# Two PSUM banks taken in turn by the first-layer tiles and the small products of an attention-and-MLP kernel

## The chip, the cores and the metric

The kernel runs on one core of one Trainium2 chip. The metric is the device time of one execution in microseconds. Before the change it is 946.12 us, the median of 3 runs (945.28 to 949.42). A difference is told as a ratio of times measured in turn on one chip.

## The reference

Two computations stand behind each other. The first is clustered attention over 4 batches, 8 heads, 768 positions and 64 dimensions: each query and each key is assigned to the nearest of 16 centroids of its head, and a query sees only the keys of its own cluster.

```
mask   = q_assign[:, :, :, None] == k_assign[:, :, None, :]
scores = where(mask, scale * q @ k.T, -1e9)
x      = softmax(scores) @ v          # 4 x 768 rows of 512
```

The second is an MLP over the 3072 rows: `h = x @ w_in` (512 to 2048), `g = s * relu(h)**2 + b`, `out = g @ w_out` (2048 to 512). Everything is float32, and the kernel keeps that accuracy by splitting numbers into two float16 halves.

## The kernel before, in words

**Units and steps.** The attention is cut into 192 units (line 459): a unit is one batch, one chunk of 256 rows, one pair of heads, one of two row tiles and one head. Step `i` of the main loop issues unit `i`: its scores (`scores`, L476), the row maximum on VectorE (L486), the exponentials on ScalarE (L493, L496), the split into halves (ScalarE L126, GpSimd L528), the turn through a DMA transpose (L530), and four steps later the product with the values (`value`, L574 to L576).

**The MLP** runs behind it by `LAG = 21` steps. Its 192 steps are 12 chunks of 256 rows times 16 slices of the 2048 hidden columns. Step `m` makes one tile `h` (`mlp_in`, L632: 12 matmuls of 128x256 into one PSUM bank), ScalarE reads it once (`mlp_relu`, L639) and squares it twice from SBUF (L641, L642), GpSimd makes the low half (`mlp_gl`, L647), and two steps later 6 matmuls add it to the chunk's accumulator (`mlp_out`, L659). The first tile of a chunk needs the chunk's four `x` tiles, which `finish_x` makes.

**The small products** prepare later units and run as generators that `background()` moves on by one stage a step. `allmax` (L101, L102) takes a maximum over partitions with one or two matmuls against the identity: its tiles are `am_q`, `am_k`, `am_v` and `am_x`. `prep_k` and `prep_q` make `pk` and `pq`, the products of keys or queries with the centroids (L357, L358, L407, L408), which VectorE reads in `onehot` (L298, L299). `column_sums` makes one tile `pb` (L287).

**PSUM** has eight banks, and all are given away: four hold two score buffers, two hold the accumulator, one has the tag `h` and one the tag `m`.

```
    ps_s = ctx.enter_context(tc.tile_pool(name="ps_s", bufs=2, space=PSUM))
    ps_a = ctx.enter_context(tc.tile_pool(name="ps_a", bufs=1, space=PSUM))
    ps_h = ctx.enter_context(tc.tile_pool(name="ps_h", bufs=1, space=PSUM))
    ps_m = ctx.enter_context(tc.tile_pool(name="ps_m", bufs=1, space=PSUM))
```

A tag with one buffer holds one tile at a time. The next tile of the tag, in the order in which the code makes them, gets the bank when the last reader of the one before has finished. From step 21 on the `h` tiles alone use tag `h`, and the small products alone use tag `m`.

**The order of the work.** The code is written step by step, and the framework's scheduler (`schedule_with_timeline_sim=True`) then orders each engine's instructions by its own model of their times: what is ready earliest in the code's order goes first, with a few groups moved up by `high_priority`. On the chip each engine works its list in that fixed order, and a waiting instruction holds up all behind it on its engine.

Of the kernel before, what the change touches and what calls it, by code (L numbers as in the profile page):

```python
# [10 lines left out]
F32 = mybir.dt.float32  # L11
# [7 lines left out]
P = 128  # L19
# [7 lines left out]
def tile_cluster_attention_mlp(ctx, tc, q, k, v, cent, w_in, w_out, s_in, b_in, out):  # L27
# [15 lines left out]
    LAG = 21  # L43
# [10 lines left out]
    ps_h = ctx.enter_context(tc.tile_pool(name="ps_h", bufs=1, space=PSUM))  # L54
    ps_m = ctx.enter_context(tc.tile_pool(name="ps_m", bufs=1, space=PSUM))
# [35 lines left out]
    def columns(n, name):  # L91
        return sb.tile([P, n], BF16, tag=f"amb{n}", name=f"amb_{name}", bufs=3)

    def allmax(dst, src, name, bank="m"):
        n = src.shape[1]
        if bank == "turned":
            pm = turned[:, 0]
        else:
            pm = (ps_m if bank == "m" else ps_h).tile([P, 512], F32, tag=bank, name=f"am_{name}")
        for j in range(n):  # L100
            nc.tensor.matmul(pm[:, j * P : (j + 1) * P], src[:, j : j + 1].broadcast_to([P, P]), identb, start=True, stop=True)  # L101
        V.tensor_reduce(dst, pm[:, : n * P].rearrange("p (n q) -> p n q", q=P), axis=AX.X, op=ALU.max)  # L102
# [74 lines left out]
    def weight_tile(name):  # L177
        return cp.tile([P, KT, P], F32, tag="w", name=name, bufs=2 * NF + 1)
# [102 lines left out]
        WSP[ft] = (made[0], made[1].rearrange("p e a f -> p e (a f)"))  # L281

    def column_sums():
        pb = ps_m.tile([P, 512], F32, tag="m", name="pb")
        for ft in range(NF):
            for e in range(2):
                nc.tensor.matmul(pb, ones16, WSP[ft][1][:, e, :], start=(ft + e == 0), stop=(ft + e == NF))  # L287
        V.tensor_tensor(glob[:, 7:8], bv, glob[:, 4:5], op=ALU.mult)
        bias.append(weight_tile("bias").rearrange("p a f -> p (a f)"))
        V.tensor_scalar(bias[0], pb, glob[:, 7:8], None, op0=ALU.mult)  # L290
# [12 lines left out]
        V.tensor_tensor(o, e, m.unsqueeze(2).broadcast_to([P, nb, C]), op=ALU.is_equal)  # L303
        eng.tensor_scalar(dst, o.unsqueeze(2).broadcast_to([P, nb, 4, C]), mul, add, op0=ALU.mult, op1=ALU.add)

    step = [0]
    START = {b: [48 * b + x for x in ((-26, -25, -23, -20) if b == 1 else (-40, -38, -32, -28))] for b in range(1, B)}

    def until(k):
# [8 lines left out]
    def prep_k(b, hp):  # L318
        kb = kb_kept
        if b == 0 and hp > 0:  # L320
            kb = sb.tile([P, 2 * T, P], F16, tag="big", name=f"kb_{hp}", bufs=BIGN).rearrange("p (h t) (e d) -> p h t e d", h=2, e=2)
        n = f"{b}_{hp}"
        kn = sb.tile([P, 2, T, D], F32, tag="kv", name=f"kn_{n}", bufs=5)
        load(kn, k[b, 2 * hp : 2 * hp + 2].rearrange("h (p t) d -> p h t d", t=T))
        yield
        if b:
            yield from until(START[b][2] if hp == 0 else step[0] + 1)
        if hp == 0:
            KSM[b] = sb.tile([P, 4, NP], F32, tag="ksm", name=f"ksm_{n}", bufs=2)
        sm = [KSM[b][:, e, hp : hp + 1] for e in range(4)]  # L330
        km = columns(1, f"k{n}")
        absmax(km, kn.rearrange("p h t d -> p (h t d)"))
        if b:
            yield
        allmax(sm[1], km, f"k{n}", "m" if b or not hp else "h")
        yield
        scale2(sm[2], sm[1])
        inverse2(V, sm[3], sm[2], 22)
        if b == 0 and hp > 0:
            ka = sb.tile([P, 2 * T, P], F16, tag="big", name=f"ka_{hp}", bufs=BIGN).rearrange("p (h t) (e d) -> p h t e d", h=2, e=2)  # L340
        else:
            ka = sb.tile([P, 2, T, 2, D], F16, tag="big", name=f"ka_{n}", bufs=BIGN)
        yield from split(ka[:, :, :, 0, :], ka[:, :, :, 1, :], kn, sm[2], False)
        G.tensor_copy(kb[:, :, :, 0, :], ka[:, :, :, 0, :])
        KA = sb.tile([P, 2 * T, P], F16, tag="KA", name=f"KA_{n}", bufs=5)
        KB = sb.tile([P, 2 * T, P], F16, tag="KB", name=f"KB_{n}", bufs=5)
        KS[(b, hp)] = (KA, KB)
        last_turn[0] = nc.sync.dma_start_transpose(KA, ka.rearrange("p h t e d -> p (h t e d)"))
        yield
        yield  # L350
        pa = (ps_m if b or not hp else ps_h).tile([P, 512], F32, tag="m" if b or not hp else "h", name=f"pk_{n}")
        for h in range(2):
            hc = slice((2 * hp + h) * C, (2 * hp + h + 1) * C)
            for t in range(T):
                i = h * T + t
                o = pa[:, i * C : (i + 1) * C]
                nc.tensor.matmul(o, KA[:, i, :], cT[:, 0, hc], start=True, stop=False)  # L357
                nc.tensor.matmul(o, KA[:, i, :], cT[:, 1, hc], start=False, stop=True)  # L358
        mk = kb.rearrange("p h t e (r c) -> p (h t) e r c", c=C)[:, :, 1, :, :]
        yield from onehot(pa, 2 * T, f"k{n}", mk, BIG, -BIG, G if b or hp > 1 else V)  # L360
        last_turn[0] = nc.sync.dma_start_transpose(KB, kb.rearrange("p h t e d -> p (h t e d)"))

    def prep_q(b, c, hq):
        n = f"{b}_{c}_{hq}"
        nh = 4
        qn = sb.tile([P, 2 * T * P // 2], F32, tag="big", name=f"qn_{n}", bufs=BIGN)[:, : nh * CT * D].rearrange("p (h t d) -> p h t d", h=nh, t=CT)
        load(
            qn, q[b, nh * hq : nh * hq + nh].rearrange("h (p t) d -> p h t d", t=T)[:, :, c * CT : (c + 1) * CT, :]
        )
        yield  # L370
        prs = slice(2 * hq, 2 * hq + 2)
        sm = sb.tile([P, 4, 2], F32, tag="qsm", name=f"qsm_{n}", bufs=3)
        qm = columns(2, f"q{n}")
        absmax(qm, qn.rearrange("p (j h) t d -> p j (h t d)", j=2))
        if b + c:
            yield
        allmax(sm[:, 1, :], qm, f"q{n}", "m" if b or c else "h")
        yield
        f = sm[:, 2, :]
        scale2(f, sm[:, 1, :])  # L380
        V.tensor_tensor(f, f, KSM[b][:, 3, prs], op=ALU.min)
        V.tensor_tensor(sm[:, 1, :], f, KSM[b][:, 2, prs], op=ALU.mult)
        inverse2(V, sm[:, 3, :], sm[:, 1, :], -3)
        qa = sb.tile([P, 2 * T * P], F16, tag="big", name=f"qa_{n}", bufs=BIGN)[:, : nh * CT * 2 * D].rearrange("p (h t e d) -> p h t e d", h=nh, t=CT, e=2)
        qb = sb.tile([P, 2 * T * P], F16, tag="big", name=f"qb_{n}", bufs=BIGN)[:, : nh * CT * 2 * D].rearrange("p (h t e d) -> p h t e d", h=nh, t=CT, e=2)
        both = []
        for j in range(2):
            hs = slice(2 * j, 2 * j + 2)
            both.append(split(qb[:, hs, :, 0, :], qa[:, hs, :, 0, :], qn[:, hs], sm[:, 2, j : j + 1], b + c == 0))
        for z in zip(*both):  # L390
            yield
        for z in both:
            next(z, None)
        G.tensor_copy(qa[:, :, :, 1, :], qb[:, :, :, 0, :])
        QA = sb.tile([P, nh * CT, P], F16, tag="QA", name=f"QA_{n}", bufs=2)
        QB = sb.tile([P, nh * CT, P], F16, tag="QB", name=f"QB_{n}", bufs=2)
        QS[(b, c, hq)] = (QA, QB, sm)
        nc.sync.dma_start_transpose(QA, qa.rearrange("p h t e d -> p (h t e d)"))
        yield
        yield  # L400
        pa = (ps_m if b or c else ps_h).tile([P, 512], F32, tag="m" if b or c else "h", name=f"pq_{n}")
        for h in range(nh):
            hc = slice((nh * hq + h) * C, (nh * hq + h + 1) * C)
            for t in range(CT):
                i = h * CT + t
                o = pa[:, i * C : (i + 1) * C]
                nc.tensor.matmul(o, QA[:, i, :], cT[:, 0, hc], start=True, stop=False)  # L407
                nc.tensor.matmul(o, QA[:, i, :], cT[:, 2, hc], start=False, stop=True)  # L408
        mk = qb.rearrange("p h t e (r c) -> p (h t) e r c", c=C)[:, :, 1, :, :]
        yield from onehot(pa, nh * CT, f"q{n}", mk, BIG, 0.0, G if b or c or hq else V)  # L410
        nc.sync.dma_start_transpose(QB, qb.rearrange("p h t e d -> p (h t e d)"))
# [213 lines left out]

    def mlp_in(b, c, ft):
        n = f"{b}_{c}_{ft}"
        ph = ps_h.tile([P, 512], F32, tag="h", name=f"h_{n}")
        GS[(b, c, ft)] = ph
        terms = [(kt, wl, xl) for kt in range(KT) for wl, xl in ((0, 0), (0, 1), (1, 0))]  # L630
        for i, (kt, wl, xl) in enumerate(terms):
            nc.tensor.matmul(ph[:, :CW], WSP[ft][0][:, wl, kt, :], XS[(b, c, kt)][:, :, xl, :],  # L632
                             start=(i == 0), stop=(i == len(terms) - 1))
# [121 lines left out]
    while i < NU + 8 or i - LAG < NS + 4:  # L755
        m = i - LAG
# [66 lines left out]
```

## Time and profile before

| what | value |
|---|---|
| median of 3 runs | 946.12 us |
| the profiled execution | 952.97 us |
| its span, first to last instruction | 951.3 us |
| TensorE (PE) busy | 830.0 us, 87% of the span |
| ScalarE (ACT), VectorE (DVE), GpSimd (POOL) busy | 75%, 68%, 58% |
| `h` matmuls, L632 | 2304 in 192 tiles |
| accumulator matmuls, L659 | 1152 |

The profiled execution takes 1.7 us more than its span, and 6.85 us more than the median of the runs. Busy time counts matmuls from start to end, and they overlap, so a short gap between two of them can be hidden. A row of the timeline has the start, the length, the engine and line, the operation, what it writes and reads and how many are merged; in brackets stand the idle time of the engine before it and what ended that.

### The profile page before, as it was taken

Reading aid. Unit: us, or ns where it says so; the run is one execution under the profiler, and the core shown is the slowest. Engines: PE = TensorE matmul, PEld = TensorE weight load, DVE = VectorE, ACT = ScalarE, POOL = GpSimd, SP = SyncE. Lnnn points to the kernel's source line nnn. Section 1 sums busy time; section 2 is a strip of 40 time slices with the busy share of each in tenths; the row PEclk is TensorE's granted clock in tenths of the full one; section 3 lists DMA queues with packets and bytes.
Section 4 is the critical chain, followed back from the end, with each engine's and each line's share of the span. In section 5 each row is a group of like instructions: output and inputs, shape, how many; then the busy total and the mean of one; then the engine's idle time right before and its main releaser. Section 6 shows DMA issues by size and latency. Waiting matters only on the chain.

```text
span 951.3 us, 22936 instructions
## 1 busy us (share of the span) xinstructions
PE 830.0 (87%) x8697; PEld 580.1 (61%) x8697; DVE 651.1 (68%) x1684; ACT 715.4 (75%) x1405; POOL 548.0 (58%) x580
## 2 busy tenths in 40 slices
PE   0565667886999889999999989999999899999997
PEld 0353445554676657767666657667766676676764
DVE  7689978798786766758967766667877565654100
ACT  3469866777688678788878868888888788888543
POOL 3010115667577567677677747767776676666321
PEclk9975697999999999999999999999999999999999
DMA  5898513767897897876887978979968777577200
GB/s 165 215 262 283 161 38 80 174 145 150 168 168 146 172 204 123 167 162 139 178 169 164 201 156 148 171 145 197 178 140 182 145 123 159 115 140 140 46 23 23
DMA packets 437759, 144.25 MB, mean 152 GB/s; under 512 B 405392, under 2 KB 434064, under 8 KB 437648
## 3 DMA queue, kind: packets, MB, share of 16 engines
q1 hardware_dynamic: 437648, 142.78, 70.7%
q8 instruction: 68, 1.11, 0.5%
q14 instruction: 43, 0.35, 0.1%
HBM read 35.69 MB, written 6.29 MB: 44 GB/s over the span
## 4 chain that ended last, share of the span: by engine, by line
PE 45%; DVE 23%; DMA 12%; ACT 7%; issue 5%; POOL 2%; SPq 1%; POOLq 0%; DVEq 0%; ACTq 0%
PE h L632 16%; PE acc L659 16%; PE sc L476 6%; DVE ssm L486 5%; DMA qn<-in_q_dram 3%; DMA PT<-ph 2%; PE sc L574 2%; DMA kn<-in_k_dram 2%; DMA vn<-in_v_dram 2%; PE sc L576 2%; PE sc L575 2%; ACT p L496 1%; DVE wis L279 1%; DVE qa L196 1%; DMA wst<-in_moe_w_in_dram 1%
## 5 line engine op out<-in xcount | busy, mean ns | idle before, releaser
L528 POOL TENSOR_TENSOR ph<-p,ph 128x768 f16<-128x768 f32 x176 | 297.0, 1688 | 129.7 <-ACT ph L126 71.1
L632 PE MATMUL h<-x,wis 128*128 128x256 f16 x2304 | 291.9, 276 | 16.1 <-ACT r L639 9.7
L659 PE MATMUL acc<-wos,gs 128*128 128x512 f16 x1152 | 299.7, 381 | 4.1 <-POOL gs L647 2.8
L632 PEld LDWEIGHTS <-wis 128*128 128x128 f16 x2304 | 222.5, 99 | 72.3 <-issue 18.0
L496 ACT ACTIVATE p<-sc,ssm,qsm 128x768 f32<-128x768 f32 x192 | 188.5, 982 | 2.0
L647 POOL TENSOR_TENSOR gs<-r,gs 128x256 f16<-128x256 f32 x192 | 136.5, 712 | 88.1 <-ACT r L642 79.4
L486 DVE TENSOR_REDUCE ssm<-sc 128x1 f32<-128x768 f32 x192 | 181.7, 947 | 2.8 <-PE sc L476 2.6
L659 PEld LDWEIGHTS <-gs 128*128 128x128 f16 x1152 | 101.4, 98 | 79.4 <-POOL gs L647 5.6
L493 ACT ACTIVATE ssm<-ssm,lift,qsm 128x1 f32<-128x1 f32 x192 | 73.1, 381 | 91.3 <-DVE ssm L486 90.1
L126 ACT ACTIVATE ph<-p 128x768 f16<-128x768 f32 x164 | 136.7, 833 | 1.3 <-DMA PT<-ph 0.2
L639 ACT ACTIVATE r<-h,cf 128x256 f32<-128x256 f32 x192 | 89.2, 465 | 57.8 <-PE h L632 54.5
L574 PE MATMUL sc<-vh,PT 128*128 128x65 f16 x1032 | 117.4, 195 | 6.9 <-DMA PT<-ph 6.8
L576 PE MATMUL sc<-vh,PT 128*128 128x65 f16 x1032 | 117.9, 193 | 0.0
L575 PE MATMUL sc<-vl,PT 128*128 128x64 f16 x1032 | 117.5, 192 | 0.0
L476 PE MATMUL sc<-KA,QA 128*128 128x384 f16 x384 | 98.9, 340 | 19.2 <-ACT p L496 13.8
L574 PEld LDWEIGHTS <-PT 128*128 128x128 f16 x1056 | 99.1, 98 | 22.8 <-DMA PT<-ph 10.1
L575 PEld LDWEIGHTS <-PT 128*128 128x128 f16 x1056 | 98.5, 99 | 11.8 <-issue 0.5
L476 PE MATMUL sc<-KB,QB 128*128 128x384 f16 x384 | 99.2, 340 | 6.9 <-DMA QB<-qb 6.9
L576 PEld LDWEIGHTS <-PT 128*128 128x128 f16 x1056 | 98.7, 97 | 1.3
L580 DVE TENSOR_SCALAR ssm<-sc 128x1 f32<-128x1 f32 x172 | 26.1, 152 | 84.5 <-PE sc L576 83.7
L642 ACT ACTIVATE r<-r 128x256 f32<-128x256 f32 x192 | 78.8, 410 | 2.9
L641 ACT ACTIVATE gs<-r 128x256 f16<-128x256 f32 x192 | 78.9, 411 | 2.7
(176 smaller groups left out, 1145.0 us busy)
## 6 DMA issues: line engine op xcount, KB each, us to landing
wst<-in_moe_w_in_dram SPq DMA_DIRECT2D x16, 512.0 KB, 5.1
kn<-in_k_dram SPq DMA_DIRECT2D x16, 384.0 KB, 4.3
qn<-in_q_dram SPq DMA_DIRECT2D x24, 256.0 KB, 3.3
vn<-in_v_dram SPq DMA_DIRECT2D x16, 384.0 KB, 4.3
out_dram<-o SPq DMA_DIRECT2D x12, 512.0 KB, 3.6
wst<-in_moe_w_out_dram SPq DMA_DIRECT2D x8, 512.0 KB, 5.7
gs<-in_moe_w_out_dram SPq DMA_DIRECT2D x8, 512.0 KB, 4.9
PT<-ph SPq DMA_TRANSPOSE x176, 3.4
```

The source lines that it names most:

```text
L126: A.activation(dst, src, AF.Copy)
L476: last_score[0] = nc.tensor.matmul(sc[:, e, :HALF], X[:, col, :], y[:, h * S + e * HALF : h * S + (e + 1) * HALF], start=st, stop=not st)
L486: last_max[0] = V.tensor_reduce(SM[i // 4][:, 0, j : j + 1], U[i]["sc"], axis=AX.XY, op=ALU.max, negate=True)
L496: last_exp[0] = A.activation(p.rearrange("p (a b) -> p a b", a=2), u["sc"], AF.Exp, bias=bi, scale=u["scale"], **total)
L528: G.tensor_tensor(u["ph"][:, 1, :], u["p"], u["ph"][:, 0, :], op=ALU.subtract)
L574: nc.tensor.matmul(o1, PT[:, kt, :], vh[:, h, kt, : D + 1], start=(kt == 0), stop=False)
L575: nc.tensor.matmul(o, PT[:, kt, :], vl[:, h, kt, :], start=False, stop=False)
L576: nc.tensor.matmul(o1, PT[:, T + kt, :], vh[:, h, kt, : D + 1], start=False, stop=(kt == T - 1))
L632: nc.tensor.matmul(ph[:, :CW], WSP[ft][0][:, wl, kt, :], XS[(b, c, kt)][:, :, xl, :], start=(i == 0), stop=(i == len(terms) - 1))
L639: A.activation(r, ph[:, :CW], AF.Relu, scale=MS[(b, c)][0])
L647: G.tensor_tensor(g[:, 1, :], r, g[:, 0, :], op=ALU.subtract)
L659: nc.tensor.matmul(acc[:, t, :], g[:, gl, rows], WSP[ft][1][:, wl, :], start=(ft == 0 and gl + wl == 0), stop=(ft == NF - 1 and gl == 1))
```

## The change

`step` moves up, and a helper `small_bank` gives out the bank. Before step 21 (`LAG`) it gives the bank that was asked for, as before. From step 21 on it gives the two banks strictly in turn, whoever asks: `h` tiles, `am`, `pk`, `pq` and `pb`.

```diff
+    step = [0]
+    newest = ["m"]
+
+    def small_bank(name, tag):
+        if step[0] >= LAG:
+            tag = "h" if newest[0] == "m" else "m"
+            newest[0] = tag
+        return (ps_m if tag == "m" else ps_h).tile([P, 512], F32, tag=tag, name=name)
+
     def allmax(dst, src, name, bank="m"):
...
-            pm = (ps_m if bank == "m" else ps_h).tile([P, 512], F32, tag=bank, name=f"am_{name}")
+            pm = small_bank(f"am_{name}", bank)
...
     def column_sums():
-        pb = ps_m.tile([P, 512], F32, tag="m", name="pb")
+        pb = small_bank("pb", "m")
...
-        pa = (ps_m if b or not hp else ps_h).tile([P, 512], F32, tag="m" if b or not hp else "h", name=f"pk_{n}")
+        pa = small_bank(f"pk_{n}", "m" if b or not hp else "h")
...
-        pa = (ps_m if b or c else ps_h).tile([P, 512], F32, tag="m" if b or c else "h", name=f"pq_{n}")
+        pa = small_bank(f"pq_{n}", "m" if b or c else "h")
...
     def mlp_in(b, c, ft):
-        ph = ps_h.tile([P, 512], F32, tag="h", name=f"h_{n}")
+        ph = small_bank(f"h_{n}", "h")
```

## Rows read from the trace of the kernel before

**Rows 1.** The page: busy time of each engine, and TensorE's granted clock in slices.
```profile
PE 830.0 (87%) x8697; PEld 580.1 (61%) x8697; DVE 651.1 (68%) x1684; ACT 715.4 (75%) x1405; POOL 548.0 (58%) x580
...
PEclk9975697999999999999999999999999999999999
```
**Rows 2.** Stretches of the span: start, end, length, busy time of each engine, granted clock.
```profile
0.00:119.00 119.00, 58.12 (x501) 42.44 (x502) 99.28 (x261) 77.67 (x155) 18.05 (x53) 0.78 0.77 217
119.00:250.00 131.00, 101.60 (x1042) 67.91 (x1041) 111.73 (x257) 92.56 (x176) 73.37 (x66) 0.90 0.57 122
250.00:850.00 600.00, 574.75 (x6340) 404.60 (x6339) 419.03 (x1105) 485.64 (x949) 416.50 (x417) 0.99 0.80 160
850.00:942.70 92.70, 92.51 (x807) 64.10 (x806) 19.66 (x60) 58.21 (x124) 39.46 (x45) 1.00 0.31 61
```
**Rows 3.** Waits of PE (us in total, times, longest): whole span, then 250 to 880.
```profile
PE h L632 <- ACT r L639: 9.7, 12, 2.5
...
PE sc L574 <- DMA PT<-ph: 6.8, 7, 1.7
PE sc L476 <- ACT p L496: 3.4, 3, 1.5
PE sc L476 <- DMA QB<-qb: 3.1, 3, 1.7
```
**Rows 4.** Timeline of one step of the last stretch, PE and ACT.
```profile
935.00 1.46 PE L659 MATMUL acc<-wos,gs 128*128 128x512 f16 x6
...
935.26 0.47 ACT L639 ACTIVATE r<-h,cf 128x256 f32<-128x256 f32 x1 [1.23 <-PE h L632]
...
936.29 1.47 PE L632 MATMUL h<-x,wis 128*128 128x256 f16 x12
```
**Rows 5.** Timeline of PE: starts of `h` tiles that waited for the relu before.
```profile
162.28 0.38 PE L632 MATMUL h<-x,wis 128*128 128x256 f16 x2 [0.28 <-ACT r L639]
...
190.64 0.38 PE L632 MATMUL h<-x,wis 128*128 128x256 f16 x2 [0.87 <-ACT r L639]
...
202.44 0.27 PE L632 MATMUL h<-x,wis 128*128 128x256 f16 x1 [1.21 <-ACT r L639]
...
555.46 2.47 PE L632 MATMUL h<-x,wis 128*128 128x256 f16 x12 [2.54 <-ACT r L639]
...
830.10 0.27 PE L632 MATMUL h<-x,wis 128*128 128x256 f16 x1 [0.62 <-ACT r L639]
```
**Rows 6.** Timeline of DVE and ACT just before the wait at 555.46.
```profile
552.36 0.95 DVE L105 TENSOR_REDUCE vm<-vn 128x1 f32<-128x768 f32 x1 [3.89 <-DMA vn<-in_v_dram]
...
554.66 0.39 ACT L493 ACTIVATE ssm<-ssm,lift,qsm 128x1 f32<-128x1 f32 x1 [7.03 <-DVE ssm L486]
```
**Rows 7.** Timeline of PE between 168 and 236: an `h` tile, and waits of small products.
```profile
170.76 1.47 PE L632 MATMUL h<-x,wis 128*128 128x256 f16 x12
...
175.93 0.29 PE L101 MATMUL am_q<-identb,amb_q 128*128 128x128 bf16 x2 [2.50 <-DVE amb_q L105]
...
217.15 0.29 PE L101 MATMUL am_q<-identb,amb_q 128*128 128x128 bf16 x2 [1.47 <-DVE amb_q L105]
...
235.35 0.19 PE L407 MATMUL pq<-cT,QA 128*128 128x16 f16 x1 [3.38 <-DMA QA<-qa]
```
**Rows 8.** Tile `h`: relus from the start to 170.5 and to 891.5.
```profile
L639 ACT ACTIVATE r<-h,cf x5: 453/455/462, 151.2 to 169.6; 128x256 f32<-128x256 f32 x5
...
L639 ACT ACTIVATE r<-h,cf x172: 450/460/477, 151.2 to 890.6; 128x256 f32<-128x256 f32 x172
```
**Rows 9.** Timeline: two small products on PE, and the relus that come after them.
```profile
562.68 0.28 PE L101 MATMUL am_q<-identb,amb_q 128*128 128x128 bf16 x2
...
566.66 0.46 ACT L639 ACTIVATE r<-h,cf 128x256 f32<-128x256 f32 x1
...
891.60 0.22 PE L101 MATMUL am_x<-identb,amb_x 128*128 128x128 bf16 x1
...
898.43 0.47 ACT L639 ACTIVATE r<-h,cf 128x256 f32<-128x256 f32 x1 [1.24 <-PE h L632]
```

More of the change, by code (lines that the diff above doesn't have):

```diff
@@ L304, in onehot @@
         eng.tensor_scalar(dst, o.unsqueeze(2).broadcast_to([P, nb, 4, C]), mul, add, op0=ALU.mult, op1=ALU.add)
-    step = [0]
     START = {b: [48 * b + x for x in ((-26, -25, -23, -20) if b == 1 else (-40, -38, -32, -28))] for b in range(1, B)}
```

## The prediction

> **What bounds the kernel now.** I read the page's busy times first, then stretches, PE's waits, and the timeline around them. PE is busiest, 830.0 us of the span, and its granted clock is near full from 150 us on [rows 1]. Its idle time lies early: 119.00 - 58.12 = 60.9 us before the MLP starts, 131.00 - 101.60 = 29.4 us while it starts, 600.00 - 574.75 = 25.3 us in the 600 us that follow, and 0.2 us from 850 to the last `h` tile [rows 2]. All the work of PE stays as it is. So the change can win only PE idle time that lies between 119 and 850 us, 54.7 us at most, and can lose only by adding some.
>
> What the single bank `h` costs directly is one row: 12 of the 192 `h` tiles wait for the relu of the tile before, 9.7 us together, 0.81 us each [rows 3]. The last stretch shows why so few do: behind a tile's 12 matmuls PE has 6 accumulator matmuls, from 935.00 to 936.29, and the relu, from 935.26 to 935.73, ends under them [rows 4]. There a second bank is worth nothing.
>
> **The change part by part.** No instruction is added or removed. What changes is whom a tile waits for. From step 21 on the code makes 192 `h` tiles and 79 small products (20 `am_q`, 20 `pq`, 12 `am_k`, 12 `pk`, 3 `am_v`, 11 `am_x`, 1 `pb`). Counting through the loops in code order, with the banks in turn, a tile's bank was held by the last tile but one. Of the 191 `h` tiles behind the first, 76 then stand behind the `h` tile two before, 64 behind a small product, and 51 still behind the `h` tile just before, because one small product lies between. Of the small products, 63 stand behind an `h` tile, which none does now, and 16 behind another small one.
>
> *The 9.7 us.* I placed the 12 waits in that count. Seven lose their cause, the first at 162.28 and the last at 830.10 [rows 5]: 3.0 us together. The rest belong to tiles that keep the same relu in front, among them the longest, 2.54 us at 555.46, 4.9 us together, and to the two at 190.64 and 202.44 [rows 5], 2.1 us, whose new predecessors, a `pq` and a `pk`, are read later than the relu was. The longest is a knock-on anyway: VectorE stood 3.89 us for a load of `v`, ScalarE 7.03 us for VectorE's maximum, and the relu behind it came late [rows 6]. I take **-3.0 us**, with 0 and -9.7 as ends, since the order will be made anew.
>
> *Other waits of PE that a freer `h` could fill.* After 250 us PE waits 6.8 + 3.4 + 3.1 = 13.3 us for turned probabilities, for a score buffer and for queries, in 13 places [rows 3]. A further `h` tile lasts 1.3 us (12 matmuls, to 1.47 with the last one's end [rows 4]), more than the mean wait of 1.0 us, so the ends are 0 and -13.3. It helps only where the scheduler puts it ahead of the waiting instruction, which it does only where its own model sees the wait. I take a quarter, **-3.3 us**.
>
> *The start of the MLP.* Between 150 and 255 us the MLP now runs ahead: 10 `h` tiles start before a small product that will hold their bank first. The one at 170.76 goes ahead of an `am_q` that waits until 175.93 for its load [rows 7]. With the change that tile must come behind it, so PE has 1.3 us less to do before a wait that stays. The waits of small products there are 2.50, 1.47 and 3.38 us [rows 7]; each can grow by a tile or so. Ends: 0, and 10 x 1.3 = 13 us. I take the three places at half a tile each, **+2.0 us**: VectorE, at 111.73 of 131 us [rows 2], holds this stretch up more than PE does.
>
> *Small products behind relus.* In the trace of before, 40 of the 63 start ahead of the relu that will stand in front of them. For the first of the worst, an `am_q` at 562.68, that relu starts at 566.66; for the last, an `am_x` at 891.60, at 898.43 [rows 9]. This order becomes impossible, and PE, which works in order, would stand with everything behind the product. But MLP tiles have room to come forward: with a bank free, most of them could start over 3 us earlier than now, and then their relus do too. Ends: 0, and 40 x 0.81 = 32 us. The nearest row is the `h` tiles' own: 12 in 192 waited, 0.81 us each [rows 3], so 63 x 12/192 x 0.81 = **+3.2 us**.
>
> *Covered, so costed at nothing:* the later readers. A late `am_q` starts the chain to the queries later, but it is begun 10 steps ahead of its unit; a step takes (891.5 - 170.5)/(172 - 5) = 4.3 us [rows 8], so 43 us of lead cover it. If that cover goes, the wait for queries, 3.1 us in 3 places after 250 us [rows 3], is what grows. No DMA is added or moved past a queue by the code itself.
>
> **The sum**: -3.0 - 3.3 + 2.0 + 3.2 = -1.1 us against the profiled execution's 952.97, that is 951.9. That execution is 6.85 us above the median of the runs; the same step from the median gives **945.0 us**. A measurement of this kernel can tell about 0.5%, 4.7 us, from no change, so the forecast is no change.
>
> What the tail shows is that PE already overlaps a tile's reading with other matmuls [rows 4]. The Trainium skill (Perfetto Trace Analysis, section Matmuls) says instead that independent groups of matmuls should rotate through different banks, so that the reading of one overlaps the next group. By it alone all of the 9.7 us would go, and the time would be 936.4. No row here shows it yet. The same skill also speaks against it (TensorE: Matmul & The Clock Gate, section HAM oscillation): in a kernel whose matmuls had been brought close together, double-buffering PSUM gave no further gain, 125.5 us after 126.6. The tail's rows agree with that one.
>
> **The rivals.**
>
> *The two banks give all that the wait's row promises* (35%). PE loses the 9.7 us of waits for the relu, because the scheduler reorders freely and my count by code order doesn't hold: 946.1 - 9.7 = 936.4 us. For it: 140 of the 191 tiles get another predecessor. Against it: the longest wait comes from a load [rows 6].
>
> *The small products become the bound, slower* (24%). The place is PE's queue, at an `am` or `pq` that stands behind a relu. It decides where the MLP lags by more than a step, 4.3 us, for then that step's own slack can't make it good. In the trace of before that holds for 12 of the 40 products, the first and last being those in [rows 9]. If these 12 each cost the mean wait of 0.81 us, that is 9.7 us, and 946.1 + 9.7 = 955.8 us. For it: every such product is in front of scores in PE's fixed order. Against it: the lag itself comes from the single bank.
>
> *PE's clock drops* (3%). More short waits could cost clock: before 250 us, where PE is idle for 29.4 of 131 us, the granted clock is 0.90, and after it 0.99 [rows 2], of which full is 2.4 GHz. If the 600 us fell to 0.97, they would take 600 x 0.02/0.97 = 12 us more: 958. Beside this stands a section of the same page on the clock gate (A second HAM failure mode: psum-queue depth-cycling): cycling through banks made PE idle briefly between groups so often that the clock swung. By it the time would be this rival's. The trace of before shows no such swing after 250 us.
>
> That the change does nothing is part of the forecast: 51 tiles keep their relu.
>
> **How the numbers follow.** Forecast, no change: 0.38. Faster by more than 0.5%: 0.35, the first rival. Slower by more than 0.5%: 0.24 + 0.03 = 0.27. The low end is 946.1 less 9.7 and a third of the 13.3, 932.0. The high end takes in the second rival and the third, 959.0. Inside it, the forecast's own range is 941 to 951.
>
> **What would show it.** In the changed kernel's PE waits the row of `h` on the relu should fall from 9.7 to about 7 us, and new rows of `am` or `pq` on the relu should come to about 3 us. In the stretches, the idle time from 119 to 250 should rise by about 2 us, and from 250 to 850 fall by about 3. The last stretch should have the same rhythm as in [rows 4]. I am wrong if the idle time of 250 to 850 falls below 17 us, or if either stretch gains over 8 us.

## The result and the profile after

The changed kernel takes 932.72 us (median of 4 runs, 931.24 to 934.60), the kernel before 947.04 beside it (4 runs, 945.28 to 949.42). The ratio is 0.9848, 95% interval 0.9818 to 0.9879: 14.3 us, or 1.5%, faster. That lies in the predicted range, 0.7 us above its low end. The forecast itself, no change, did not come. The first rival's side did, by more than its price.

The profiled executions differ by more than the medians: 952.97 us before and 932.08 after, spans of 951.3 and 930.3. The one before stood 5.9 us above its median. So a comparison of the two traces explains 21.0 us, and some 6 of them are that execution's own.

The page of the changed kernel answers to [rows 1]:

```profile
PE 824.4 (89%) x8697; PEld 578.9 (62%) x8697; DVE 631.4 (68%) x1684; ACT 711.7 (77%) x1405; POOL 546.4 (59%) x580
...
PEclk9976697999999999999999999999999999999999
```

The instruction counts are the same. PE's idle time is 930.3 - 824.4 = 105.9 us, against 951.3 - 830.0 = 121.3: 15.4 us less, near the 14.3 us between the medians. The other 5.6 us are PE's busy time, for the same matmuls; more on them below. The stretches of the changed kernel (columns as in [rows 2]) say where:

```profile
0.00:119.00 119.00, 60.18 (x528) 44.08 (x528) 100.08 (x262) 78.46 (x158) 18.78 (x53) 0.81 0.78 218
119.00:250.00 131.00, 103.43 (x1052) 69.37 (x1053) 106.83 (x252) 91.28 (x171) 73.85 (x66) 0.90 0.62 126
250.00:850.00 600.00, 585.38 (x6492) 413.89 (x6491) 410.53 (x1128) 498.88 (x983) 425.79 (x426) 1.00 0.82 163
850.00:924.00 74.00, 74.00 (x625) 51.08 (x623) 12.51 (x41) 43.12 (x95) 27.78 (x36) 1.00 0.19 46
```

Idle PE time falls from 60.9 to 58.8 us before 119, from 29.4 to 27.6 up to 250, and from 25.3 to 14.6 in the 600 us that follow [rows 2]. The last of these, 10.6 us, is the gain's place. The granted clock of those 600 us goes from 0.99 to 1.00. The waits of PE there, in the changed kernel from 250 to 880 us (total, times, longest), answer to [rows 3]:

```profile
PE h L640 <- ACT r L647: 3.3, 5, 1.6
PE sc L582 <- DMA PT<-ph: 3.2, 6, 0.7
PE sc L484 <- DMA QB<-qb: 2.5, 3, 1.9
PE pq L415 <- DMA QA<-qa: 1.7, 2, 1.4
...
PE sc L484 <- ACT p L504: 1.0, 2, 0.7
PE h L640 <- DVE qsm L111: 0.5, 1, 0.5
PE pq L415 <- ACT r L650: 0.2, 1, 0.2
```

The wait for the relu went from 9.7 us in 12 places to 3.3 in 5; no such wait is left before 250 us. The three waits that the prediction called fillable went from 6.8 + 3.4 + 3.1 = 13.3 to 3.2 + 1.0 + 2.5 = 6.7. No small product waits for a relu: the last row names the second squaring (L650), and at that place, 598.75 us, the newest relu had ended at 597.12. Part of the saving came back as another wait: an `h` tile that stands behind a small product waits for that product's reader on VectorE. The changed kernel's waits from 119 to 250:

```profile
PE pq L415 <- DMA QA<-qa: 5.7, 2, 3.8
...
PE h L640 <- DVE vm L111: 1.9, 1, 1.9
...
PE h L640 <- DVE oe_q L308: 0.9, 1, 0.9
PE h L640 <- DVE bias L299: 0.7, 1, 0.7
PE h L640 <- DVE ksm L111: 0.4, 1, 0.4
```

Those four and the `qsm` row above make 4.4 us, in five places.

The same two small products as in [rows 9] show what happened to the order. In the changed kernel's timeline the relu stands ahead of both:

```profile
546.80 0.45 ACT L647 ACTIVATE r<-h,cf 128x256 f32<-128x256 f32 x1
...
548.91 0.28 PE L110 MATMUL am_q<-identb,amb_q 128*128 128x128 bf16 x2
...
878.57 0.47 ACT L647 ACTIVATE r<-h,cf 128x256 f32<-128x256 f32 x1 [1.47 <-PE h L640]
...
880.91 0.22 PE L110 MATMUL am_x<-identb,amb_x 128*128 128x128 bf16 x1
```

Before, the products came 4 and 7 us ahead of these relus [rows 9]. The MLP has come forward: by 891.5 us 180 relus have started, 172 before [rows 8].

The 5.6 us of busy time are not shown to be the change's. The mean granted clock is 0.954 in the profiled execution before and 0.961 in the one after. But the kernel before ran 66 more times beside the experiments below, with a mean of 0.959 (0.948 to 0.969), and the four runs of the changed kernel have 0.957 to 0.965, mean 0.960. So the execution profiled before had a low clock for its kernel. In three orders of the old banks (the kernel before, e4 and e12 below) PE is busy for 830.0, 824.7 and 828.4 us, and in three of the turn (the changed kernel, e8 and e3) for 824.4, 827.2 and 827.6: these overlap. PE's idle times over the span don't: 121.3, 117.6 and 125.0 against 105.9, 104.3 and 111.8. The page of e4, with a clock of 0.961:

```profile
PE 824.7 (88%) x8697; PEld 578.4 (61%) x8697; DVE 639.7 (68%) x1684; ACT 715.0 (76%) x1405; POOL 546.3 (58%) x580
```

One place in the trace of before does show what a lower clock costs. In [rows 5] the tile at 555.46, behind the longest wait, took 2.47 us for its 12 matmuls; [rows 4] has 1.47 for the same 12. The kernel before there (PE alone: busy time, count, clock, DMA):

```profile
550.00:565.00 15.00, 12.46 (x112) 0.89 0.61 144
```

This wait was paid twice, once as idle time and once as matmuls at half clock behind it. From 250 to 924 us the changed kernel's clock has no such dip. Another strict turn has one (e8 below: 0.89 from 595 to 610).

### The profile page after: what moved, and what is told of

Its sections match the earlier page's. It is cut to its first block, busy times and chain, and to the rows that moved or that the text cites. A ratio compares the mean times of both kernels' runs of the same rounds, so it can differ in the third digit from the quotient of the medians.

```text
span 930.3 us, 22973 instructions
## 1 busy us (share of the span) xinstructions
PE 824.4 (89%) x8697; PEld 578.9 (62%) x8697; DVE 631.4 (68%) x1684; ACT 711.7 (77%) x1405; POOL 546.4 (59%) x580
## 4 chain that ended last, share of the span: by engine, by line
PE 43%; DVE 18%; DMA 14%; ACT 8%; issue 6%; POOL 5%; SPq 2%; DVEq 0%; ACTq 0%; POOLq 0%
PE acc L667 15%; PE h L640 15%; PE sc L484 6%; DVE ssm L494 4%; DMA qn<-in_q_dram 3%; DMA PT<-ph 3%; DMA vn<-in_v_dram 3%; POOL ph L536 2%; DMA kn<-in_k_dram 2%; PE sc L582 2%; PE sc L584 2%; PE sc L583 2%; ACT p L504 2%; POOL gs L655 2%; SPq L538 1%
## 5 line engine op out<-in xcount | busy, mean ns | idle before, releaser
L667 PE MATMUL acc<-wos,gs 128*128 128x512 f16 x1152 | 295.8, 381 | 2.0 <-POOL gs L655 1.6
L640 PEld LDWEIGHTS <-wis 128*128 128x128 f16 x2304 | 223.6, 98 | 80.1 <-issue 14.6
L582 PE MATMUL sc<-vh,PT 128*128 128x65 f16 x1032 | 113.5, 196 | 3.4 <-DMA PT<-ph 3.2
L583 PE MATMUL sc<-vl,PT 128*128 128x64 f16 x1032 | 113.3, 193 | 0.0
L584 PE MATMUL sc<-vh,PT 128*128 128x65 f16 x1032 | 113.0, 194 | 0.0
L650 ACT ACTIVATE r<-r 128x256 f32<-128x256 f32 x192 | 78.5, 410 | 2.8
```

The costliest lines, as they stand in the source:

```text
L582: nc.tensor.matmul(o1, PT[:, kt, :], vh[:, h, kt, : D + 1], start=(kt == 0), stop=False)
L583: nc.tensor.matmul(o, PT[:, kt, :], vl[:, h, kt, :], start=False, stop=False)
L584: nc.tensor.matmul(o1, PT[:, T + kt, :], vh[:, h, kt, : D + 1], start=False, stop=(kt == T - 1))
L667: nc.tensor.matmul(acc[:, t, :], g[:, gl, rows], WSP[ft][1][:, wl, :], start=(ft == 0 and gl + wl == 0), stop=(ft == NF - 1 and gl == 1))
```

## The experiments

The edits are to `small_bank` of the changed kernel unless another is named. A ratio is to the kernel before, which ran on the same chip beside it (medians of 947.7 to 948.9 us). "Idle" is PE's idle time from 250 to 850 us of the run's profile: 600 less its busy time. A **direct pair** is a tile made, in the order of the code, right behind the tile made just before it and in that tile's bank; it is counted over the 271 tiles from step 21 on. The kernel before has 126 `h` behind `h` and 14 small behind small, 140; strict turn has none.

Theory A: the gain is the `h` tile freed from the relu before it. Theory B: the scheduler's order was made anew and happened to be a good one. Theory C puts the gain on the small products' change of bank.

**Only the `h` tiles take turns (e1).** The small products stay in `m`.

```diff
-        if step[0] >= LAG:
+        if step[0] >= LAG and name.startswith("h_"):
```

> From step 21 on only the h tiles take the two banks in turn; every small product stays in bank m. Theory A (the gain comes from h tiles that no longer stand behind the relu of the tile just before): ratio to before 0.98 to 0.99, PE's wait of h on the relu 4 us or less. Theory B (the new order of the work is luck, any new order moves the time by one or two per cent either way): anything from 0.98 to 1.02, with no relation to that wait. Theory C (the small products gain, because they get a second bank): ratio within 0.5% of 1.00.

962.65 us, ratio 1.0145 [1.0120, 1.0171]. Its steady stretch, and its waits from 250 to 880:

```profile
250.00:850.00 600.00, 567.30 (x6194) 399.70 (x6192) 399.78 (x1079) 479.16 (x939) 405.99 (x409) 0.98 0.78 157
```

```profile
PE sc L582 <- DMA PT<-ph: 7.2, 6, 2.9
PE sc L484 <- ACT p L504: 7.1, 7, 2.1
PE h L640 <- DVE oe_k L308: 3.8, 2, 2.0
PE h L640 <- DMA x<-xn: 3.7, 2, 2.7
...
PE h L640 <- ACT r L647: 2.6, 2, 2.2
```

The relu wait is as small as in the changed kernel, 2.6 us, and the kernel is slower than before. In theory A's plain form that can't be. The longest rows are those of the turned probabilities and of the score buffer, 7.2 and 7.1 us. Behind them `h` waits 3.8 us for a VectorE reader of a small product: those share bank `m` with every second `h` tile.

**Only the small products take turns (e2).** The `h` tiles stay in `h`.

```diff
-        if step[0] >= LAG:
+        if step[0] >= LAG and not name.startswith("h_"):
```

> From step 21 on only the small products take the two banks in turn; every h tile stays in bank h. Theory A: no gain, ratio 0.997 to 1.02, PE's wait of h on the relu stays near 9 us or grows. Theory B: anything from 0.98 to 1.02. Theory C: ratio 0.98 to 0.99.

994.04 us, ratio 1.0475 [1.0446, 1.0504]. Its steady stretch and two of its waits:

```profile
250.00:850.00 600.00, 547.54 (x5908) 378.68 (x5907) 375.66 (x1035) 457.85 (x888) 388.58 (x390) 0.98 0.75 152
```

```profile
PE sc L484 <- ACT p L504: 13.4, 13, 2.6
PE h L640 <- ACT r L647: 8.8, 15, 1.3
```

Theory C falls. The wait that grows most is the scores' for their buffer, from 3.4 us before to 13.4; the relu's row goes from 7.4 to 8.8. How the small products in `h` bring the first about, the rows don't show. Neither half of the change gains anything alone.

**The turn begins with the other bank (e3).** The rule and the pairs are the same, but each tile's bank is the other one.

```diff
-    newest = ["m"]
+    newest = ["h"]
```

> The changed kernel with the turn begun at the other bank: every tile has the same predecessors as in the changed kernel except the first ones, and the order of the work is made anew. Theory A: the gain stays, ratio 0.98 to 0.99. Theory B: the gain may be gone, 0.98 to 1.02.

942.44 us, ratio 0.9934 [0.9912, 0.9956], idle 16.1 us: a gain, but less than half of the changed kernel's, and outside theory A's range. Between the two traces lie 9.1 us: 4.3 of idle time from 119 to 250 (31.9 against 27.6), 1.4 from 250 to 850, and 3.2 of PE's busy time.

**The old banks, another order (e4).** In the kernel before, the product with the values has another priority, so the scheduler's order is made anew.

```diff
-            with tc.high_priority(offset=100):
+            with tc.high_priority(offset=110):
```

> The kernel before, banks untouched; the priority offset of the value products is 110 in place of 100, which changes half of PE's order and says nothing about banks. Theory A: within 0.7% of 1.00, and PE's wait of h on the relu stays at 7 to 12 us. Theory B: moves by over 1% either way.

948.27 us, ratio 1.0003 [0.9978, 1.0027], idle 22.3. The waits for the relu fell from 9.7 us to 4.9 in 7 places, below theory A's 7 to 12, and the time stayed, against theory B's 1%. From 250 to 880 us:

```profile
PE h L632 <- ACT r L639: 2.5, 4, 0.9
```

That is less than the changed kernel's 3.3, and the three waits called fillable come to 5.4 + 2.4 + 1.4 = 9.2 us in place of 13.3. So a new order alone, with the old banks, can shrink these rows. It gave no time here.

**A small product in the newest `h` tile's bank (e5), or in the other one (e6).** In both, the `h` tiles take turns among themselves. In e5 the direct pairs are 65 small behind `h`; in e6 they are 65 `h` behind small. Both keep 14 small behind small.

e5:

```diff
-            tag = "h" if newest[0] == "m" else "m"
-            newest[0] = tag
+            if name.startswith("h_"):
+                newest[0] = "h" if newest[0] == "m" else "m"
+            tag = newest[0]
```

e6:

```diff
             tag = "h" if newest[0] == "m" else "m"
-            newest[0] = tag
+            if name.startswith("h_"):
+                newest[0] = tag
```

> From step 21 on the h tiles take strict turns among themselves, and a small product takes the bank of the newest h tile, so it stands directly behind that tile's relu; the next h tile is free, and the one after it stands behind the small product with one h tile between. Theory D1 (what costs is an h tile directly behind a small product, as in the run where small products kept bank m): such a pair never occurs, so ratio 0.98 to 0.99, as the changed kernel or better. Theory D2 (what costs is a small product directly behind a relu): ratio 1.005 to 1.03.

> From step 21 on the h tiles take strict turns among themselves, and a small product takes the other bank than the newest h tile, so the next h tile in code order always stands directly behind the small product. Theory D1: ratio 1.01 to 1.05, with PE waits of h on VectorE's readers of small products of over 5 us from 119 to 880. Theory D2: ratio 0.98 to 0.99, since no small product stands directly behind a relu.

e5: 950.68 us, ratio 1.0029 [1.0013, 1.0045]. e6: 951.66, ratio 1.0047 [1.0025, 1.0069]. The steady stretch and the waits of e5:

```profile
250.00:850.00 600.00, 575.36 (x6344) 404.71 (x6341) 396.41 (x1108) 483.31 (x952) 414.61 (x417) 0.99 0.81 160
```

```profile
PE sc L485 <- DMA QB<-qb: 5.0, 4, 1.8
PE sc L485 <- ACT p L505: 5.0, 9, 1.1
PE pk L366 <- ACT r L648: 2.7, 3, 1.3
...
PE h L641 <- ACT r L648: 2.4, 2, 1.8
```

And of e6:

```profile
250.00:850.00 600.00, 572.65 (x6360) 406.47 (x6358) 408.55 (x1109) 484.79 (x957) 415.16 (x418) 1.00 0.81 161
```

```profile
PE sc L583 <- DMA PT<-ph: 5.0, 6, 1.3
PE sc L485 <- DVE cf L630: 3.4, 2, 1.8
PE acc L668 <- POOL gs L656: 3.0, 3, 2.4
...
PE h L641 <- DVE oe_k L309: 1.8, 2, 1.6
...
PE h L641 <- ACT r L648: 0.3, 2, 0.2
```

Both rotate the `h` tiles, both lose a little, and all four ranges of D1 and D2 are missed. If one of the two mixed kinds of pair were all that costs, the kernel without that kind would have gained; neither did. And e6 has hardly a wait for a relu left (0.3 us) with 27.4 us idle: its losses stand in other rows, for `PT`, for `cf`, for `gs`, for loads. So in e6 the bank's own wait is not where the cost of the layout shows. The wait rows of e6 prove no mechanism for it either.

**The turn from step 64 on (e7), or from step 21 to 63 alone (e10).**

e7, then e10:

```diff
-        if step[0] >= LAG:
+        if step[0] >= 64:
```

```diff
-        if step[0] >= LAG:
+        if LAG <= step[0] < 64:
```

> The turn of the changed kernel from step 64 on only; the steps before keep one bank for each. If the gain is spread over the steps as PE's idle time in the two profiles is (of about 12 us less idle time, 5 before unit 64 and 7 behind it): ratio 0.990 to 0.994. If it comes from the start of the MLP: 0.997 to 1.003. If from the later steps alone: 0.984 to 0.988.

> The turn of the changed kernel in steps 21 to 63 only. If the gains of the two parts add: the changed kernel's ratio less that of the turn from step 64 on, so 0.990 to 0.995. If the later part needs the earlier one: 0.996 to 1.003.

e7: 941.31 us, ratio 0.9924 [0.9903, 0.9944]. e10: 953.01, ratio 1.0055 [1.0030, 1.0079]. The parts don't add up: e10 misses both of its ranges. Stretches 250 to 350 and 350 to 850 (PE alone) separate them. The kernel before, then the changed one, then e7, then e10:

```profile
250.00:350.00 100.00, 92.69 (x1018) 0.98 0.84 168
350.00:850.00 500.00, 482.06 (x5325) 1.00 0.80 159
```

```profile
250.00:350.00 100.00, 98.02 (x1079) 1.00 0.89 172
350.00:850.00 500.00, 487.36 (x5420) 1.00 0.81 161
```

```profile
250.00:350.00 100.00, 93.66 (x1036) 0.98 0.85 169
350.00:850.00 500.00, 487.60 (x5395) 1.00 0.79 160
```

```profile
250.00:350.00 100.00, 97.31 (x1071) 1.00 0.86 175
350.00:850.00 500.00, 474.20 (x5265) 1.00 0.79 157
```

e10 has the changed kernel's early stretch, 2.7 us idle against 7.3 before, and then, back in the old layout, 25.8 us idle where the kernel before has 17.9. Its unit 80 still starts its exponentials at 419.0 us, as in the changed kernel, and at 429.6 before; the lead is lost later. How much of the 25.8 us is luck of that order stays open: three other orders of the old layout have 15.2 (e4), 17.9 and 21.6 (e12). e7 has the opposite pair: 6.3 us early, as before, and 12.4 late, as after.

**The changed kernel in another order (e8).** The priority of the values goes from 100 to 60.

```diff
-            with tc.high_priority(offset=100):
+            with tc.high_priority(offset=60):
```

> The changed kernel with the priority offset of the value products at 60 in place of 100: the same banks and predecessors, another order on PE. If the gain belongs to the banks: ratio 0.982 to 0.994. If it was luck of one order: 0.995 to 1.02.

936.04 us, ratio 0.9883 [0.9863, 0.9904], idle 15.5. The gain outlasts a new order.

**All in one bank (e9).** From step 21 on every tile takes `h`, so all 270 pairs are direct.

```diff
-            tag = "h" if newest[0] == "m" else "m"
-            newest[0] = tag
+            tag = "h"
```

> From step 21 on every h tile and every small product takes bank h, and bank m is empty. Theory D3 (a tile made directly behind another in the same bank costs, whichever kinds they are, and the strict turn is the only layout of those tried with no such pair): all 270 tiles behind the first are such pairs, so this is the slowest of all, ratio above 1.05 and PE idle time from 250 to 850 above the 52 us of the run in which only small products took turns. If instead what cost in that run was that small products changed banks: ratio 1.00 to 1.04.

1028.57 us, ratio 1.0843 [1.0822, 1.0863]. Its steady stretch and its waits:

```profile
250.00:850.00 600.00, 538.30 (x5720) 366.16 (x5721) 354.59 (x1000) 444.81 (x855) 374.28 (x379) 0.98 0.76 145
```

```profile
PE sc L483 <- ACT p L503: 17.5, 26, 1.0
PE sc L581 <- DMA PT<-ph: 12.7, 14, 3.0
PE sc L483 <- DMA QB<-qb: 12.6, 4, 4.5
PE h L639 <- ACT r L646: 8.2, 10, 3.0
```

Even here the relu costs `h` only 8.2 us directly. All waits at the bank, with those of `h` for readers on VectorE and those of small products, come to 20.3 us. The scores wait 17.5 us for their buffer and 12.6 for their queries, and the products with the values 12.7 for their turned probabilities. D3's forecast came out; why the scores pay so much, no run shows.

**The turn from the first product on (e11).** The two products made before step 21, `pw` and `px`, also go through `small_bank`.

```diff
-        if step[0] >= LAG:
+        if True:
...
-            pw = ps_h.tile([P, 512], F32, tag="h", name=f"pw_{ft}")
+            pw = small_bank(f"pw_{ft}", "h")
...
-        px = ps_m.tile([P, 512], F32, tag="m", name=f"px_{i}")
+        px = small_bank(f"px_{i}", "m")
```

> The changed kernel with the strict turn from the first product on, the weights' row sums and the early value products included. If the rule holds for the start too: 0.975 to 0.984, with less PE idle time than 60 us before 119 us. If the start is held up by loads and by VectorE alone: 0.983 to 0.990, as the changed kernel.

940.38 us, ratio 0.9923 [0.9896, 0.9950], above both ranges. Its steady stretch is the best of all, 10.7 us idle:

```profile
250.00:850.00 600.00, 589.29 (x6525) 415.76 (x6523) 421.23 (x1128) 498.56 (x980) 429.61 (x430) 1.00 0.83 165
```

It loses that at the start: unit 16's exponentials come at 143.7 us, at 132.6 in the changed kernel. Over the whole span PE idles as long as there (105.1 us, 105.9) and is busy 9.2 us longer. Why, no run shows.

**The old banks, a third order (e12).** As e4, with 150.

```diff
-            with tc.high_priority(offset=100):
+            with tc.high_priority(offset=150):
```

> The kernel before with the priority offset of the value products at 150 in place of 100: one bank for each, a third order of the work. If the old layout itself holds PE's idle time in its later steps up: PE idle from 350 to 850 us of 15 to 26 us (17.9 in the kernel before, 25.8 in the run with the turn in steps 21 to 63 only), ratio 0.995 to 1.01. If the old layout can do as well in a lucky order: idle time of 14 us or less, ratio 0.985 to 0.993.

954.50 us, ratio 1.0061 [1.0037, 1.0085]. So three orders of the old layout give 0, 0 and +0.6%, and three of strict turn (changed kernel, e8, e3) -1.5, -1.2 and -0.7%. The order is worth up to some 0.9%, and the groups don't overlap.

**Together.**

| run | direct pairs | idle, us | ratio |
|---|---|---|---|
| changed kernel | 0 | 14.6 | 0.985 |
| e8, another order | 0 | 15.5 | 0.988 |
| e3, other bank first | 0 | 16.1 | 0.993 |
| e11, turn from the start | 0 | 10.7 | 0.992 |
| e7, turn from step 64 | mixed | 18.7 | 0.992 |
| e4, another order | 140 | 22.3 | 1.000 |
| kernel before | 140 | 25.3 | 1 |
| e5 | 79 | 24.6 | 1.003 |
| e6 | 79 | 27.4 | 1.005 |
| e12, a third order | 140 | 27.6 | 1.006 |
| e10, turn to step 63 | mixed | 28.5 | 1.006 |
| e1 | 79 | 32.7 | 1.015 |
| e2 | 192 | 52.5 | 1.048 |
| e9 | 270 | 61.7 | 1.084 |

Each idle time is that of one profiled execution. PE's idle time in the steady part ranks the runs nearly as the ratios do; e11, which pays at the start, is the plain exception. By stretches, wherever strict turn holds it is lower than wherever it doesn't. From 250 to 350 it is 1.8 to 2.7 us with it (changed kernel, e3, e8, e10, e11) and 6.1 to 7.3 in the old layout (before, e4, e7, e12). From 350 on it is 8.9 to 14.0 with it (changed kernel, e3, e7, e8, e11) and 15.2 to 25.8 in the old layout (before, e4, e10, e12), so there the nearest two lie 1.2 us apart. The other layouts have 3.9 to 10.9 and 19.8 to 50.8. The wait of `h` for the relu ranks nothing: over the whole span it is 0.8 us in e6, which loses, and 8.1 in e7, which gains.

What is shown: under strict turn PE idles less, in either part of the run, and the whole kernel is faster in each of three orders. Why it idles less is not shown. Luck of the order (theory B) sets how much, as far as three orders on each side can tell. What fits, without being proved: a layout kept up without direct pairs of any kind gains, the others don't (theory D3, in e9's expectation). **What stays open**: the number of pairs doesn't rank the layouts alone, as e1 with 79 is slower than the kernel before with 140. Bank `m` holds 175 of the 271 tiles there, which may be the reason; that wasn't tried. e5 and e6 also share 14 pairs of small products, and no run had the mixed pairs without those.

## Why the prediction was wrong in its likeliest case

**What bounds the kernel: right.** The gain came from PE's idle time: 15.4 us less between the two traces, 12.5 of them in the 54.7 us between 119 and 850, and 14.3 between the medians. "Can win only PE idle time" held: no gain in busy time is shown beyond that of other orders.

**The 9.7 us: the step that failed.** "Seven lose their cause" gave -3.0 us; the row fell by 9.7 - 3.3 = 6.4. The step placed the 12 waits of the old order on the new predecessors and let a wait stay wherever its relu stays, 4.9 us, or where a later reader replaces it, 2.1. The count of predecessors held: counted in the code's order, the five waits that are left all belong to tiles that still stand behind the `h` tile just before. The places didn't: of the 12 tiles that waited, one waits for a relu again, for 0.47 us at 682.87. The step itself said that "the order will be made anew" and then used the old one's waits. Its parts also make 3.0 + 4.9 + 2.1 = 10.0 us, 0.3 over the row; counted again, six of the 12 lose their relu (2.9 us), four keep it (4.8) and two get a `pq` and a `pk` (2.1).

**Other waits: mis-sized by two.** A quarter, -3.3, was taken; half went, 13.3 - 6.7 = 6.6 us. With the 4.1 us that the relu's row loses after 250 us (7.4 of its 9.7 before, 3.3 now) this makes 10.7, as much as the stretch's gain of 10.6; the other rows of PE's waits nearly cancel there, 4.1 us before and 3.8 now. That a freer `h` filled these waits, as the step had it, no row shows, and e4 shrinks the same rows with the old banks.

**The start: the wrong sign.** +2.0 was predicted, and the stretch gained 1.8 us. Some cost is there: `pq`'s wait for its load grew from 3.4 to 5.7, as predicted, the scores' for their buffer from 2.7 to 5.6, and `h` waits 3.9 us for readers on VectorE. What the sum left out are waits that went: two at the `am_q` of [rows 7], 2.50 and 1.47, and 2.4 us for the relu, of which it had let 2.1 stay.

**Small products behind relus: nothing in place of +3.2.** No small product waits for a relu. The reason given against the rival held: the tiles came forward, and the relu in front of each of the 63 small products is done when the product's turn comes. The price moved to `h` tiles behind small products, a pair that the prediction counted (64) and gave no term: 4.4 us in five places. The cover for the queries held, 2.5 us after 3.1.

**The rivals.** "All that the wait's row promises", 936.4 of 946.1, ratio 0.990, came nearest, and the measured 0.985 [0.982, 0.988] lies beyond it; the three orders of strict turn have 0.985, 0.988 and 0.993. Its reason held in part: the row lost 6.4 of its 9.7, and waits elsewhere gave the rest. The rule behind it (the Trainium skill, Perfetto Trace Analysis, section Matmuls), that independent groups of matmuls should rotate through different banks, points the way this kernel moved; but e1, e5 and e6 rotate the `h` tiles too and lose, so it decides nothing without the banks' other users. What the Trainium skill reports on the other side, of another kernel (TensorE: Matmul & The Clock Gate, section HAM oscillation), no further gain from double-buffering PSUM, is not what the changed kernel shows (0.985). The rival "small products become the bound" did not happen in the changed kernel; e2, at +4.8%, has 35 small products right behind an `h` tile in its bank, but its rows don't show that they are what costs. The clock's rival didn't come: in the steady stretch 0.99 became 1.00.

That the measured time lies inside the range is in part luck. The low end stood for all of the 9.7 us and a third of the 13.3; what came was 6.4 us of the one and half of the other, and another order of the same turn (e3) gains some 0.9% less.

The prediction's own tests said it: wrong if the idle time from 250 to 850 falls below 17 us (14.6), or a stretch gains over 8 (10.6).

## What to carry to other kernels

Where few PSUM banks serve several kinds of tiles, look at the order in which the code makes all of them, not at one kind's wait: a turn over all users gained 0.7 to 1.5% here, and four rules that turn for one kind alone cost 0.3 to 4.8%. When a scheduler makes the order anew, don't count which waits of the old order survive; take the whole row as one end, and try two or three orders before a difference under 1% is put down to an edit. Before a difference in busy time is put down to an edit too, look at other executions and orders: the one profiled before had a low clock, and over three orders the busy times of old and new overlap. A long wait of PE can carry a second price, half-clock matmuls behind it, as at 555.46 in the kernel before; it need not, as e1's clock stayed at 1.00 from 310 to 325 us, around a wait of 2.67.

## What the runs showed that was not expected

Two banks for everything beat one bank for each by 1.5%, while four other ways to share the same two banks were slower than one for each. Much of a layout's cost does not show at the bank: in e6 all waits of `h` for a reader of its bank come to under 3 us of 27.4 idle, and in e9, where all tiles share one bank, the waits at it come to some 20 us of 61.7.
